# Weight signs carried by a parametric ReLU, and state-times-r matmuls grouped ahead of column-tiled ones

## The chip, the core and the metric

The kernel runs on one core of a Trainium2 chip. The time is device microseconds of that core, from three executions: 1002.29 us median, 1002.23 to 1002.87. One execution, taken by the hardware profiler, gives the trace that this document reads.

## What is computed

A decayed linear attention over 4 x 8 heads of 768 steps and width 48 gives 3072 tokens of 384 features. Two blocks with 2048 hidden features follow, one with a squared ReLU, one with h - tanh(h). The four weight matrices come as float64.

```python
def _attn_ref(r, k, v, w, u):
    for t in range(S):
        cur = np.einsum('bhd,bhe->bhde', u[None] * kt, vt)
        y[:, :, t] = np.einsum('bhd,bhde->bhe', rt, state + cur)
        state = w[None, :, :, None] * state + np.einsum('bhd,bhe->bhde', kt, vt)

def _moe_ref(x, w_in, w_out):
    r = np.maximum(x @ w_in, 0.0)
    return r * r @ w_out

def _moe2_ref(x, w_in, w_out):
    h = x @ w_in
    return (h - np.tanh(h)) @ w_out
```

## The kernel before

The 3072 tokens are six blocks j of 512 tokens: one chunk of 128 time steps, for four batches. A block runs through the attention, then through layer 1. Layer 2 starts when layer 1 is over. A unit of a layer is one slice f of 128 hidden features (16 per block) and one block: `gemm1` (L489, nine matmuls into `h`), an activation (`act1` or `act2`), and `gemm2_1` (L516) or `gemm2_2` (L594). Every fp32 product is a sum of three products of high and low parts, so activations and weights are split in two: `glo` and `xs` are such low parts, made on GpSimd (L507, L549) or VectorE (L583).

**Weights.** The slabs, 32 of them (16 per layer), each hold one f of w_in and w_out as pairs of 32-bit words. `load_w` brings one in (768 KB, buffer `raw`); `conv0` on ScalarE (L84) multiplies the high word, read as float32, by 2^-112, which moves the exponent's offset from float64's to float32's; `conv1` on VectorE puts the words together: L89 shifts the low word, L90 joins the high word shifted left by 3, and L93 adds the sign bit. `conv2` rounds the result on ScalarE (L101) to the high weight part, and GpSimd (L102) subtracts it for the low part; in layer 2 it also asks for the slab five further on. Layer 1's slabs 0 to 2 are converted in the start, slabs 3 to 15 in block 0 (slab f+3 by unit f). Layer 2's slabs 1 to 15 are converted in block 5 of layer 1 (slab f+1 by unit f; slab 0 shortly before). A unit's `gemm1` needs L101 and L102 of its slab.

**Attention.** Blocks 1 to 5 are made while blocks 0 to 4 are in layer 1, in half steps d: half of the heads of one chunk of one batch, eight per block, 40 in all. `att_c(d)` writes the half step's output `y` for two pairs of heads z: L418 multiplies the state `sbd` by r (112 rows by 112 columns of the array), L422 adds the part from within the chunk with two matmuls of 48 columns each, in two places of the array (column tiling). L431 makes the state's addition. Then `att_e(d)` takes `y` out (L448 on ScalarE, L450 on VectorE) and updates the state (L456). GpSimd makes the diagonal of `am` (L320); VectorE fills `am` with L338 or L331.

The order on each engine is written out by hand, in the loop from L762. A unit n first issues `conv2`, then the first half of a unit two or three ahead, then `conv1`, the attention's half step, and the second half of unit n.

```python
        if layer == 1 and j == 0:
            conv1(1, f + 3)
        if att:
            att_c(d)
            att_e(d)
            loads(d)
            pack(d)
        if layer == 1 and j == NB - 1 and 0 < f < NF - 1:
            conv2(2, f - 1)
```

Of the kernel before, what the change touches and what calls it, by code (L numbers as in the profile page):

```python
# [7 lines left out]
F32 = mybir.dt.float32  # L8
# [4 lines left out]
AF = mybir.ActivationFunctionType  # L13
ALU = mybir.AluOpType
# [11 lines left out]
def decay_attention_moe_moe_kernel(  # L26
# [10 lines left out]
    nc = tc.nc  # L37
    NTAU, GP, _, NP, C = rk.shape
# [22 lines left out]
    def bank(i, name):  # L61
        return ps.tile([128, 512], F32, tag=f"bank{i}", name=name)
# [14 lines left out]
    def words(layer, f):  # L77
        raw = raw_t[layer, f]
        return raw[:, :, 0], raw[:, :, 1]

    def conv0(layer, f):
        if f < NF:
            lo, hi = words(layer, f)
            nc.scalar.activation(out=hi.bitcast(F32), in_=hi.bitcast(F32), func=AF.Copy, scale=2.0 ** -112)  # L84

    def conv1(layer, f):
        if f < NF:
            lo, hi = words(layer, f)
            nc.vector.tensor_scalar(out=lo, in0=lo, scalar1=29, scalar2=None, op0=ALU.logical_shift_right)  # L89
            nc.vector.scalar_tensor_tensor(  # L90
                out=lo, in0=hi, scalar=3, in1=lo, op0=ALU.logical_shift_left, op1=ALU.bitwise_or
            )
            nc.vector.scalar_tensor_tensor(  # L93
                out=lo, in0=hi, scalar=0x80000000, in1=lo, op0=ALU.bitwise_and, op1=ALU.bitwise_or
            )

    def conv2(layer, f):
# [20 lines left out]
    sbd = [ac.tile([GP, NP, GP], F32, name=f"sbd{o}") for o in range(TPB)]  # L118
# [10 lines left out]
    rk_t = {}  # L129
# [277 lines left out]
    def att_c(d):  # L407
        i, e = divmod(d, 2)
        j, o = divmod(i, TPB)
        if j not in xt:  # L410
            xt[j] = xp.tile([128, 2, KK, TB], F32R, tag="x", name="xt")
        kn, vn = kv_t[i][:, 0], kv_t[i][:, 1]
        am = am_t.pop(d)
        y = bank(6 if d > 2 * ND and d % 2 else 7, "y")
        yv = y[:, 0:2 * C].rearrange("p (P t) -> p P t", P=2)
        for z in range(2):
            p = 2 * e + z
            nc.tensor.matmul(  # L418
                yv[0:GP, z, :], lhsT=sbd[o][:, p, :], rhs=rk_t[i][:, 0, p, :], start=True, stop=False
            )  # L420
            for a in (1, 0):
                nc.tensor.matmul(  # L422
                    yv[64 * a:64 * a + D, z, :], lhsT=vn[:, 2 * p + a, :], rhs=am[:, 2 * a + z, :],
                    start=False, stop=True,
                )
        pv = y[:, 2 * C:2 * C + 2 * D].rearrange("p (P x) -> p P x", P=2)
        if j != NCH - 1:
            for z in range(2):
                for a in (1, 0):
                    h = 4 * e + 2 * z + a  # L430
                    nc.tensor.matmul(  # L431
                        pv[64 * a:64 * a + D, z, :], lhsT=kn[:, h, :], rhs=vn[:, h, :], start=True, stop=True
                    )
        y_t[d] = (yv, pv)
# [209 lines left out]
    with tc.manual_schedule():  # L644
# [57 lines left out]
        for i in range(TPB):  # L702
# [21 lines left out]
            if i == 0:  # L724
                conv0(1, 0)
                conv1(1, 0)
                conv2(1, 0)
            if i == 1:
                conv0(1, 1)
                att_r(4, G)  # L730
                att_u(5, G)
            if i == 2:
                conv1(1, 1)
            if i == 3:
                conv2(1, 1)
        load_w(1, 3)
        conv0(1, 2)
        rs(4)
        att_d(ND)
# [4 lines left out]
        att_b(ND)  # L744
        att_k(4, G)
        conv1(1, 2)
        att_m(ND)
        load_w(1, 4)
# [13 lines left out]
        for n, (layer, j, f) in enumerate(units):  # L762
# [14 lines left out]
# [5 lines that stand above are left out]
# [108 lines left out]
```

## Time and profile before

| | us |
|---|---|
| median of the runs | 1002.29 |
| profiled execution, own time | 1001.29 |
| its span, first to last instruction | 999.3 |
| PE busy | 943.1 (94%) |
| VectorE (DVE) busy | 777.5 (78%) |
| ScalarE (ACT) busy | 642.6 (64%) |
| GpSimd (POOL) busy | 351.9 (35%) |

Busy time is a mean over stages with different limits. PE is TensorE's matmuls, PEld its weight loads, which lie beside them; matmuls overlap each other in these rows, so their durations add up to more than the time they take. In the chain of waits each matmul counts only with the time that it adds. "issue" is time in which an engine waits for nothing that the profile shows.

### The profile page before, as it was taken

The page shows a single profiled execution, that of the slowest core. Times are in us where ns is not written, and L with a number is a line of the kernel's source. Part 1 is how long each engine was busy: PE and PEld are TensorE (multiplying, and loading weights), DVE is VectorE, ACT ScalarE, POOL GpSimd, SP SyncE. Part 2 cuts the span into 40 slices and gives each one's busy share as a digit, 9 for nine tenths or more (in the row PEclk, how much of TensorE's full clock was granted, in tenths as well). Part 3 has the DMA queues.
Part 4 walks back from the last instruction along what each step waited for, and adds up shares of the span by engine and source line. Part 5 has one row for each costly group of instructions (what it writes and reads, how often), then busy time and mean ns, then how long its engine had stood idle before and what let it go on. Part 6 is the DMA issues. An engine that isn't in the chain of part 4 may idle for free.

```text
span 999.3 us, 14270 instructions
## 1 busy us (share of the span) xinstructions
PE 943.1 (94%) x5036; PEld 788.6 (79%) x5036; DVE 777.5 (78%) x1181; ACT 642.6 (64%) x1157; POOL 351.9 (35%) x267
## 2 busy tenths in 40 slices
PE   6788879999999999999998969999999999999997
PEld 6566657888788888877886758888888898898896
DVE  7999995763674477262189999999999999999996
ACT  3444545554554554544477667888788888888885
POOL 6855665654455455353268911101001001001000
PEclk7999989999999999999999979999999999999999
DMA  8734431211221213110434310010010010100000
GB/s 240 221 126 157 142 110 51 74 56 46 73 88 50 74 51 90 36 47 9 162 128 156 127 53 11 1 53 11 1 53 11 22 33 11 53 11 1 32 1 31
DMA packets 29671, 67.56 MB, mean 68 GB/s; under 512 B 5025, under 2 KB 15137, under 8 KB 29601
## 3 DMA queue, kind: packets, MB, share of 16 engines
q1 hardware_dynamic: 29456, 66.47, 20.9%
q8 instruction: 39, 0.64, 0.3%
q10 hardware_dynamic: 144, 0.20, 0.1%
q14 instruction: 32, 0.25, 0.1%
HBM read 55.25 MB, written 9.44 MB: 65 GB/s over the span
## 4 chain that ended last, share of the span: by engine, by line
PE 68%; DVE 17%; ACT 6%; issue 5%; DMA 2%; POOL 2%; SPq 0%; DVEq 0%; POOLq 0%; ACTq 0%
PE h L489 30%; PE acc L516 16%; PE o L594 15%; DVE raw L90 3%; PE y L422 2%; PE sc L286 2%; PE y L418 2%; DVE raw L89 2%; DVE hy L574 1%; DVE hy L573 1%; DVE hy L572 1%; ACT ghi L582 1%; DVE hy L567 1%; DMA kvt<-in_nat_dram 1%; DVE am L338 1%
## 5 line engine op out<-in xcount | busy, mean ns | idle before, releaser
L489 PE MATMUL h<-xt,w 128*128 128x512 f32 x864 | 217.6, 395 | 6.1 <-ACT w L101 3.1
L489 PE MATMUL h<-xs,w 128*128 128x512 f32 x864 | 215.4, 393 | 0.0
L594 PE MATMUL o<-w,ghi 128*128 128x384 f32 x768 | 198.4, 339 | 7.8 <-ACT x2s L532 4.9
L516 PE MATMUL acc<-ghi,w 128*128 128x512 f32 x576 | 202.5, 406 | 0.0
L489 PEld LDWEIGHTS h<-xt,w 128*128 128x128 f32 x864 | 160.0, 190 | 43.2 <-POOL w L102 5.1
L507 POOL TENSOR_TENSOR glo<-g,ghi 128x512 fp32r<-128x512 f32 x96 | 141.4, 1472 | 146.8 <-ACT ghi L506 110.1
L489 PEld LDWEIGHTS h<-xs,w 128*128 128x128 f32 x864 | 161.2, 188 | 29.5
L594 PEld LDWEIGHTS o<-w,ghi 128*128 128x128 f32 x768 | 141.6, 189 | 18.1 <-ACT x2s L532 5.4
L503 ACT ACTIVATE g<-h 128x512 f32<-128x512 f32 x96 | 57.1, 595 | 152.6 <-PE h L489 151.1
L594 PE MATMUL o<-w,glo 128*128 128x384 f32 x384 | 132.5, 345 | 8.6 <-DVE glo L583 8.3
L516 PEld LDWEIGHTS acc<-ghi,w 128*128 128x128 f32 x576 | 110.8, 192 | 25.8 <-issue 1.3
L549 POOL TENSOR_TENSOR xs<-x2f,xs 128x512 fp32r<-128x512 f32 x18 | 24.1, 1337 | 293.6 <-DVE xs L548 292.4
L516 PE MATMUL acc<-glo,w 128*128 128x512 f32 x288 | 115.0, 399 | 5.3 <-POOL glo L507 5.3
L582 ACT ACTIVATE ghi<-hy 128x512 fp32r<-128x512 f32 x96 | 60.8, 634 | 53.8 <-DVE hy L574 52.7
L102 POOL TENSOR_TENSOR w<-raw,w 128x768 fp32r<-128x768 f32 x32 | 68.0, 2126 | 54.6 <-ACT w L101 54.6
L269 DVE TENSOR_TENSOR fr<-rkt,fr 112x256 fp32r<-112x256 f32 x30 | 39.2, 1305 | 61.7 <-ACT fr L268 60.6
L594 PEld LDWEIGHTS o<-w,glo 128*128 128x128 f32 x384 | 72.5, 189 | 15.5 <-DVE glo L583 13.5
L574 DVE COPY_PREDICATED hy<-mask,th 128x512 f32<-128x512 uint8 x96 | 71.8, 748 | 10.2 <-ACT q L568 0.5
L573 DVE SCALAR_TENSOR_TENSOR hy<-q,hy 128x512 f32<-128x512 f32 x96 | 68.1, 710 | 10.4 <-ACT q L568 0.5
L567 DVE SCALAR_TENSOR_TENSOR hy<-h,y 128x512 f32<-128x512 f32 x96 | 66.3, 690 | 8.6 <-ACT ghi L582 0.5
L320 POOL TENSOR_TENSOR am<-ident,bt 128x512 f32<-128x512 f32 x44 | 50.1, 1139 | 59.6 <-DVE bt L304 56.5
L565 ACT ACTIVATE y<-h 128x512 f32<-128x512 f32 x96 | 56.9, 593 | 21.8 <-PE h L489 21.5
(104 smaller groups left out, 1498.3 us busy)
## 6 DMA issues: line engine op xcount, KB each, us to landing
raw<-in_w_dram SPq DMA_DIRECT2D x32, 768.0 KB, 4.3
rkt<-in_rk_dram SPq DMA_DIRECT2D x23, 448.0 KB, 4.3
kvt<-in_nat_dram SPq DMA_DIRECT2D x23, 384.0 KB, 4.6
x2d<-x2s SPq DMA_DIRECT2D x18, 256.0 KB, 2.3
x2f<-x2d SPq DMA_DIRECT2D x18, 256.0 KB, 2.8
out_dram<-ob SPq DMA_DIRECT2D x24, 192.0 KB, 2.0
rnt<-in_nat_dram SPq DMA_DIRECT2D x23, 192.0 KB, 2.5
xt<-ys SPq DMA_DIRECT2D x120, 16.0 KB, 1.8
```

The lines of the kernel that those rows point to most:

```text
L102: nc.gpsimd.tensor_tensor(d[:, 1], t, d[:, 0].bitcast(F32), op=ALU.subtract)
L320: nc.gpsimd.tensor_tensor(am_t[d].rearrange("p (a z) t -> p a z t", a=2), ident[:, None, None, :].to_broadcast([128, 2, 2, C]), hd.to_broa ...
L489: nc.tensor.matmul(h, lhsT=w_in(layer, f, part, kk), rhs=x[:, xpart, kk, :], start=(n == 0), stop=(n == 3 * KK - 1),)
L503: nc.scalar.activation(out=g, in_=h, func=AF.Relu)
L507: nc.gpsimd.tensor_tensor(lo, g, hi.bitcast(F32), op=ALU.subtract)
L516: nc.tensor.matmul(acc[j][m], lhsT=w_out(1, f, part, m * 128, (m + 1) * 128), rhs=g, start=(f == 0 and n == 0), stop=(f == NF - 1 and n == 2),
L565: nc.scalar.activation(out=y, in_=h, func=AF.Square)
L567: nc.vector.scalar_tensor_tensor(out=hy, in0=h, scalar=PK, in1=y, op0=ALU.mult, op1=ALU.mult)
L573: nc.vector.scalar_tensor_tensor(out=hy, in0=q2, scalar=PD, in1=hy, op0=ALU.add, op1=ALU.mult)
L574: nc.vector.copy_predicated(hy, mask, th)
L582: nc.scalar.activation(out=hi, in_=hy, func=AF.Copy)
L594: nc.tensor.matmul(acc[j][m][:, 0:DM], lhsT=g[:, m * 128:(m + 1) * 128], rhs=w_out(2, f, part, 0, DM), start=(f == 0 and n == 0), stop=(f ...
```

## The change

ScalarE's copy with scale 2^-112 becomes a parametric ReLU with the same scale and a slope of 2^32 for negative numbers. A negative high word so gets 32 added to its exponent, which sets bit 28, and the shift by 3 on VectorE carries bit 28 into the sign's place. L93 is dropped. In `att_c` both L418 matmuls of a half step come first and the four L422 after them; only the first starts the accumulation of its bank.

```diff
     def conv0(layer, f):
-            nc.scalar.activation(out=hi.bitcast(F32), in_=hi.bitcast(F32), func=AF.Copy, scale=2.0 ** -112)
+            nc.scalar.activation(
+                out=hi.bitcast(F32), in_=hi.bitcast(F32), func=AF.Prelu,
+                scale=2.0 ** -112, alpha=2.0 ** 32,
+            )
     def conv1(layer, f):
...
-            nc.vector.scalar_tensor_tensor(
-                out=lo, in0=hi, scalar=0x80000000, in1=lo, op0=ALU.bitwise_and, op1=ALU.bitwise_or
             )
     def att_c(d):
         for z in range(2):
             p = 2 * e + z
             nc.tensor.matmul(
-                yv[0:GP, z, :], lhsT=sbd[o][:, p, :], rhs=rk_t[i][:, 0, p, :], start=True, stop=False
+                yv[0:GP, z, :], lhsT=sbd[o][:, p, :], rhs=rk_t[i][:, 0, p, :], start=(z == 0), stop=False,
+                skip_group_check=True,
             )
+        for z in range(2):
+            p = 2 * e + z
             for a in (1, 0):
                 nc.tensor.matmul(
                     yv[64 * a:64 * a + D, z, :], lhsT=vn[:, 2 * p + a, :], rhs=am[:, 2 * a + z, :],
-                    start=False, stop=True,
+                    start=False, stop=True, skip_group_check=True,
                 )
```

In the changed file L89 and L90 are L92 and L93, and the matmuls of L422, L431, L489, L516 and L594 stand three lines further down. The orders on ScalarE, GpSimd and SyncE are the same before and after, instruction by instruction; ScalarE's has one table load in both, ahead of its first activation (L171).

VectorE before, in block 0: the conversion of a slab, the half step's evacuation behind it, and the next slab.

```order
L250 TENSOR_TENSOR rkt<-rkt,tr 112x256
L89 TENSOR_SCALAR raw<-raw 128x768
L90 SCALAR_TENSOR_TENSOR raw<-raw 128x768
L93 SCALAR_TENSOR_TENSOR raw<-raw 128x768
L450 TENSOR_TENSOR xt<-y,xt 112x2x128
L456 SCALAR_TENSOR_TENSOR sbd_87<-sbd_87,wdec,y 48x48 x4
```

The same place in the change:

```order
L250 TENSOR_TENSOR rkt<-rkt,tr 112x256
L92 TENSOR_SCALAR raw<-raw 128x768
L93 SCALAR_TENSOR_TENSOR raw<-raw 128x768
L453 TENSOR_TENSOR xt<-y,xt 112x2x128
L459 SCALAR_TENSOR_TENSOR sbd_87<-sbd_87,wdec,y 48x48 x4
```

The third operation on `raw` is gone, 32 times; nothing else on VectorE moves.

PE before, one half step between the first half of a unit (`h`) and the second half of another:

```order
L489 MATMUL h<-xt,w_2_556 128x512 x9
L418 MATMUL y<-rkt,sbd_87 112x128
L422 MATMUL y<-am,kvt 48x128 x2
L418 MATMUL y<-rkt,sbd_87 112x128
L422 MATMUL y<-am,kvt 48x128 x2
L431 MATMUL y<-kvt 48x48 x4
```

And in the change:

```order
L492 MATMUL h<-xt,w_2_553 128x512 x9
L418 MATMUL y<-rkt,sbd_87 112x128 x2
L425 MATMUL y<-am,kvt 48x128 x4
L434 MATMUL y<-kvt 48x48 x4
L519 MATMUL acc_610<-ghi,w_1_501 128x512
```

The second L418 now stands ahead of the column-tiled matmuls; the number of matmuls is the same.

## Rows read from the trace of the kernel before

**Rows 1.** Busy time in stretches: length, PE, PEld, DVE, ACT, POOL, clock, DMA, GB/s.
```profile
47.00:150.00 103.00, 85.30 (x465) 61.23 (x461) 95.86 (x134) 48.68 (x78) 61.59 (x40) 0.92 0.41 134
150.00:478.00 328.00, 327.56 (x1862) 265.13 (x1862) 182.07 (x341) 166.02 (x333) 162.26 (x135) 1.00 0.19 57
...
502.70:577.60 74.90, 70.35 (x298) 56.18 (x296) 70.35 (x44) 54.40 (x80) 62.39 (x31) 0.98 0.39 134
577.60:592.00 14.40, 5.19 (x15) 4.53 (x15) 13.61 (x21) 8.84 (x16) 0.00 (x0) 0.65 0.27 91
592.00:990.00 398.00, 392.57 (x1945) 348.36 (x1943) 369.63 (x572) 329.74 (x575) 23.21 (x17) 1.00 0.06 19
```

**Rows 2.** Busy time of L93 alone, in the start and in block 0.
```profile
0.00:47.00 47.00, 3.55 (x3) 0.85 0.82 236
47.00:147.00 100.00, 16.12 (x14) 0.91 0.43 138
```

**Rows 3.** Timeline of VectorE, start and block 0: start, duration, instruction, [idle before, releaser].
```profile
32.95 1.43 DVE L338 COPY_PREDICATED am<-low,sc 128x256 f32<-128x256 uint32 x4 [1.73 <-POOL am L320]
...
66.92 0.96 DVE L93 SCALAR_TENSOR_TENSOR raw<-raw 128x768 uint32<-128x768 uint32 x1
...
79.17 1.91 DVE L93 SCALAR_TENSOR_TENSOR raw<-raw 128x768 uint32<-128x768 uint32 x1
81.00 0.41 DVE L450 TENSOR_TENSOR xt<-y,xt 112x256 fp32r<-112x256 f32 x1
...
84.06 0.78 DVE L338 COPY_PREDICATED am<-low,sc 128x256 f32<-128x256 uint32 x2 [1.24 <-POOL am L320]
```

**Rows 4.** Timeline of GpSimd in block 0, beside the L93 at 79.17.
```profile
78.34 1.93 POOL L507 TENSOR_TENSOR glo<-g,ghi 128x512 fp32r<-128x512 f32 x1
```

**Rows 5.** Timeline of PE in block 0.
```profile
82.37 0.44 PE L418 MATMUL y<-rkt,sbd 112*112 112x128 f32 x2 [3.04 <-DVE sbd L456]
```

**Rows 6.** The chain that ended last, block 1: start, time added, engine, line, count.
```profile
175.88 2.07 PE h L489 x9
...
193.12 2.07 PE h L489 x9
```

**Rows 7.** The same chain, one half step.
```profile
301.79 0.22 PE y L418 x2
302.01 0.36 PE y L422 x4
302.36 0.40 PE y L418 x2
302.76 0.36 PE y L422 x4
...
305.58 0.72 PE sc L286 x6
```

**Rows 8.** Timeline of the weight loads (PEld), the second L418 of a half step.
```profile
171.87 0.27 PEld L418 LDWEIGHTS y<-rkt,sbd 112*112 112x112 f32 x2 [0.18 <-issue]
```

**Rows 9.** Timeline of VectorE in block 5: one slab, and layer 2's first activation.
```profile
547.99 2.21 DVE L89 TENSOR_SCALAR raw<-raw 128x768 uint32<-128x768 uint32 x1
550.30 1.86 DVE L90 SCALAR_TENSOR_TENSOR raw<-raw 128x768 uint32<-128x768 uint32 x1
552.20 2.52 DVE L93 SCALAR_TENSOR_TENSOR raw<-raw 128x768 uint32<-128x768 uint32 x1
...
577.88 0.68 DVE L567 SCALAR_TENSOR_TENSOR hy<-h,y 128x512 f32<-128x512 f32 x1
```

**Rows 10.** Timeline of GpSimd beside that slab.
```profile
547.21 2.57 POOL L102 TENSOR_TENSOR w<-raw,w 128x768 fp32r<-128x768 f32 x1
549.75 1.60 POOL L507 TENSOR_TENSOR glo<-g,ghi 128x512 fp32r<-128x512 f32 x1
551.30 2.58 POOL L102 TENSOR_TENSOR w<-raw,w 128x768 fp32r<-128x768 f32 x1
```

**Rows 11.** Timeline of ScalarE in block 5, a slab that comes late.
```profile
542.85 0.94 ACT L84 ACTIVATE raw<-raw 128x768 f32<-128x768 f32 x1 [4.20 <-DMA raw<-in_w_dram]
```

**Rows 12.** Groups by line, all of the execution: count, busy us, mean ns, idle before.
```profile
L171 ACT ACT_TABLE_LOAD x1 | 1.3, 1283 | 6.9 <-DMA vtab<-in_w_dram 6.9
```

More of the change, by code (lines that the diff above doesn't have):

```diff
@@ L91, in conv1 @@
                 out=lo, in0=hi, scalar=3, in1=lo, op0=ALU.logical_shift_left, op1=ALU.bitwise_or
-            )
-            nc.vector.scalar_tensor_tensor(
-                out=lo, in0=hi, scalar=0x80000000, in1=lo, op0=ALU.bitwise_and, op1=ALU.bitwise_or
             )
```

## The prediction

> **What bounds the kernel now.** I read the busy time by stretches first, since 94% for PE is a mean over stages that end on different things. From 150 to 478 us PE is busy for 327.56 of 328 us [rows 1]: there only less matmul time helps. From 592 to 990 us it is busy for 392.57 of 398 [rows 1], so what comes earlier at 592 comes earlier at the end. In between lie two stretches that PE does not fill: block 0, from 47 to 150 us, with 17.7 us without a matmul, and block 5 with the passage into layer 2, from 502.7 to 592 us, with 4.55 + 9.21 = 13.8 us [rows 1]. In both VectorE is full: 95.86 of 103 us, 70.35 of 74.9, 13.61 of 14.4 [rows 1]. These are the two stretches in which slabs are converted.
>
> Then I read who waits there. In block 0 VectorE's instructions follow each other without a gap but for one of 1.24 us per three units, for GpSimd's `am` [rows 3], and PE waits for VectorE: 3.04 us until L456, which stands behind L89, L90 and L93 in VectorE's order [rows 5]. In block 5 VectorE runs late: layer 2's first activation starts at 577.88 [rows 9], straight behind slab 14's L93.
>
> Then why L93 lasts 0.96 us in one place, 1.91 or 2.52 in another [rows 3, 9]. At 79.17 GpSimd is in L507, which ends at 78.34 + 1.93 = 80.27 [rows 4]; L93 ends 0.81 us after that. In block 5 this holds at every step: L102 ends at 549.78, L89 0.42 us later; L507 ends 1.15 after that, L90 0.81 later, the next L102 1.72 later, L93 0.84 later [rows 9, 10]. The two engines take turns on these instructions: the one that comes second stands until the other's instruction is over. A slab and a unit's L507 so need 0.42 + 0.81 + 0.84 + 1.15 + 1.72 = 4.94 us one behind the other.
>
> **The change, part by part.** The sum is made against the profiled execution's own 1001.29 us (span 999.3), 1.0 us under the median of 1002.29.
>
> *Start.* Two L93 are gone before block 0's first one, which starts just ahead of 47 us: 3.55 - 0.14 = 3.4 us busy [rows 2]. What the first gives falls into a wait, since at 32.95 VectorE has already waited 1.73 us for GpSimd's `am` [rows 3]. The second has no wait behind it: half of the sum, 1.7 us. Bounds 0 and 3.4.
>
> *Block 0.* From there to 146 us 13 more are gone; the last, at 146.74, frees nothing that PE waits for. Their time is 16.12, plus 0.14 of the first that lies before 47 us, less 0.26 of the last: 16.0 us [rows 2]. An instruction starts about 0.08 us before the one ahead of it ends (81.00 against 81.08 [rows 3]), so 16.0 - 13 x 0.08 = 14.9 us of VectorE's order. What is late next? PE's own pace with attention is 193.12 - 175.88 = 17.24 us per three units [rows 6]; VectorE's is now 23.5 (the wait at 84.06 has its like in each such period) and becomes 23.5 - (0.88 + 0.88 + 1.83) = 19.9, still the longer. ScalarE, busy 48.68 of 103 us, and GpSimd, 61.59 [rows 1], have room. So I count all 14.9. Low end: where L93 stood for GpSimd, the next instruction stands instead, and each L93 gives only its own 0.88: 13 x 0.88 = 11.4. High end: the 17.7 us that PE is idle. I take 14.9 because what follows a long L93 is L450 and L456, which read PSUM, and L450 after the long one lasts 0.41 [rows 3]. The Trainium skill (SBUF — State Buffer, "Who interferes with whom") says that VectorE is held by GpSimd only in instructions with two SBUF inputs or in a two-port mode; by it the wait is not passed on to L450, which gives the 14.9, and otherwise 11.4. The turns in block 5 agree with it; no row shows an L450 under a GpSimd instruction.
>
> *Blocks 1 to 4, the matmuls.* In the chain a half step is 0.22 for the first L418 pair of passes, 0.36 for four passes of L422, then 0.40 and 0.36 again [rows 7]. The second L418 is 0.18 dearer than the first, and 0.18 is the time that its weight load stands with nothing shown to wait for [rows 8]: the array has just held column-tiled weights. Grouped, this is paid for nowhere: 0.18 less. A second saving is the other turn: full-width passes with 256 columns add 0.72 / 6 = 0.12 [rows 7], so 128 columns 0.06, four L422 0.24, and the 0.12 left in each 0.36 is the turn to column tiling; one of two goes. Together 0.18 to 0.30 per half step; I take 0.27, nearer the upper end, since both turns are seen in the rows. 32 half steps lie where PE is the bound (blocks 1 to 4; the eight of block 0 are hidden by VectorE): 8.6 us, bounds 5.8 and 9.6.
>
> *Block 5 and the passage.* Before, 14 slabs took turns for 14 x 4.94 = 69.2 of the 74.9 us. After, a slab and an L507 need 4.10, so 57.4 us: 11.8 less, and less than the 70.35 that PE needs [rows 1]. PE becomes the bound again, its 4.55 us of idle time goes, and layer 2's first activation no longer stands behind late slabs but behind its own `h`, so the 9.21 go too, nearly. PE's clock is 0.65 in that last stretch [rows 1]: 5.19 x 0.35 = 1.8 us come back where it is full. So at most 13.8 + 1.8 = 15.6; I take 14. Low end 8: the 9.21, less a part of it that remains. Slab 15 alone, converted in between, gives 0.9 of this.
>
> *ScalarE.* The parametric ReLU does the same 768 elements as the copy. No row shows one; the nearest is L84 itself with 0.94 us [rows 11]. Between nothing and 0.94 more it stays hidden: ScalarE has 74.9 - 54.40 = 20.5 us free for 14 slabs, 1.46 each, in block 5, its tightest place [rows 1]. I count 0.
>
> Sum: 1.7 + 14.9 + 8.6 + 14 = 39.2. 1001.29 - 39.2 = 962.1 for a profiled execution, 1.0 more for a median: **963 us**. All low ends together (0 + 11.4 + 5.8 + 8 = 25.2) give 977, all high ends (3.4 + 17.7 + 9.6 + 15.6 = 46.3) give 956.
>
> **The rivals.**
>
> *The slabs' loads become the bound.* At 542.85 ScalarE stands 4.20 us for a slab that has not landed [rows 11], and everything behind it on ScalarE, the activation of layer 1 included, is late. The load is asked for by the L102 of five slabs before. If the loads stay as late as now, block 5 keeps its 4.55 us and a like delay hits the passage: block 5 gives 5 instead of 14, 972 us. Against it: L102 itself is late now because it takes turns with L93. In block 0 no such wait has a row.
>
> *The second weight load is not hidden.* If the second L418's weights cannot come in while the first L418 runs, the second costs 0.40 as now, and only the turn to column tiling is saved: 0.12 x 32 = 3.8 instead of 8.6, 968 us. The first L418's two passes together add only 0.22, though each loads its weights, and six passes of L286 add 0.72 [rows 7], which speaks against it. The Trainium skill (TensorE: Matmul & The Clock Gate, Part 3, "The mechanism") has loads overlap running matmuls only where the row groups differ; both L418 use the same 112 rows, so that rule gives this rival's 968 us. The rows of L418 and L286 do not bear it out.
>
> *Slower: the parametric ReLU is dear on ScalarE.* Its function could need another table than the copies, squares and tanh around it, and so a load before and one after, 32 times, where now there is one of 1.283 us [rows 12]. The price decides from about 3.5 us per slab: in block 5 ScalarE has 15.95 us free beside PE's 70.35 (1.14 per slab), in block 0, shortened to 88 us, 39.4 (3.0 per slab), and 14 x (3.5 - 1.14) + 13 x (3.5 - 3.0) = 39.5 us eats all the gain. Two loads alone, 2.57 us, add 14 x 1.43 = 20: 983 us, still faster. With as long again for the engine to empty each time, 5.1 us, they add 14 x 3.96 + 13 x 2.1 = 83: 1046 us. Against it: ScalarE's order in the change holds one table load, in the same place. The Trainium skill (ScalarE: Activation LUTs, "What ACT_TABLE_LOAD costs") puts load and drain at 2.66 us; by that two would be 5.3 us per slab and the time about 1051; no run here shows such a drain.
>
> *The half steps in the wrong place.* That the grouping does nothing at all (971.6 us) needs the turns to be unavoidable; the row of 0.18 us speaks against it. I count it to the case of the weight load.
>
> **How the numbers follow.** The forecast, with its own range 956 to 977, has 0.76; the loads 0.11; the weight load 0.07; the dear activation 0.03; 0.03 are left for what no row shows, a third of it slower and a third without effect. The first three all lie within 956 to 977; I widen a little on both sides for the median, to 954 and 978, and leave out well under 2 in 10. A measurement of this kernel can tell about 0.2%, 2 us, from no change. Faster by more than that 0.95, within it 0.01, slower 0.04.
>
> **What would show it.** In the changed profile VectorE's busy time should fall by about 48 us in all, in block 0 each three units should take about 20 us, and PE's idle time between 47 and 135 us should be some 15 us lower. A half step in the chain should read 0.44 for four passes of L418 and about 0.6 for eight of L422; 0.62 for the L418 would be the weight load's case. Layer 1's last block should run without a wait for L507, and layer 2's first L567 should start right behind its `h`. A row for the parametric ReLU over 2 us, or ACT_TABLE_LOAD more than once, would be the slower case; waits of L84 for `raw` of 4 us in block 5, the loads'. The forecast is wrong if VectorE still runs without a gap in block 5, or if PE has new waits in blocks 1 to 4.

## The result and the profile after

| | before | after |
|---|---|---|
| median of the runs, us | 1002.32 | 961.58 (961.38 to 963.43) |
| profiled execution, us | 1001.29 | 961.58 |
| its span, us | 999.3 | 959.6 |
| PE busy, us | 943.1 | 922.6 |
| VectorE busy, us | 777.5 | 742.4 |

The ratio is 0.9597, with a 95% interval of 0.958 to 0.9613. The forecast was 963 us.

First the page of the changed kernel, its busy times and span:

```profile
span 959.6 us, 14238 instructions
...
PE 922.6 (96%) x5036; PEld 784.3 (82%) x5036; DVE 742.4 (77%) x1149; ACT 643.0 (67%) x1157; POOL 346.1 (36%) x267
```

Next, busy time by stretches of the changed kernel, with the columns of [rows 1]. The stretches hold about the same pieces of work as those of [rows 1], at their new times: block 0 with a little of the start ahead of it, blocks 1 to 4, block 5, the passage into layer 2, and layer 2.

```profile
44.60:133.20 88.60, 79.96 (x470) 58.15 (x468) 81.17 (x121) 47.05 (x77) 64.97 (x43) 0.96 0.54 171
133.50:451.00 317.50, 316.88 (x1858) 264.68 (x1860) 190.93 (x340) 165.71 (x331) 160.80 (x134) 1.00 0.19 59
476.00:541.00 65.00, 64.82 (x286) 53.27 (x285) 51.03 (x34) 51.41 (x76) 56.57 (x30) 1.00 0.45 155
541.00:555.00 14.00, 9.64 (x34) 7.89 (x33) 13.24 (x19) 11.48 (x21) 1.87 (x1) 0.76 0.28 94
555.00:953.00 398.00, 391.10 (x1945) 348.58 (x1944) 370.15 (x572) 330.58 (x575) 23.30 (x17) 1.00 0.06 19
```

Block 5 now has 0.18 us without a matmul, where there were 4.55, and VectorE is busy for 51.03 of 65 us there: it is no longer the bound. The passage keeps 14 - 9.64 = 4.4 us of idle PE, where there were 9.2. Block 0 keeps 88.6 - 79.96 = 8.6 where there were 17.7.

Where the time went is read best from the start of the same piece of work in both traces. A unit's second half begins with its first matmul of L516 (now L519), in layer 2 of L594 (now L597):

| start of | before | after | ahead, us |
|---|---|---|---|
| block 0 | 51.50 | 49.13 | 2.37 |
| block 0, last unit | 160.54 | 143.64 | 16.90 |
| block 1 | 166.23 | 149.00 | 17.22 |
| block 5 | 502.69 | 475.97 | 26.72 |
| block 5, last unit | 571.30 | 537.71 | 33.60 |
| layer 2 | 582.59 | 544.81 | 37.78 |
| layer 2, block 1 | 659.46 | 620.61 | 38.84 |
| end of the span | 999.35 | 959.64 | 39.7 |

So 2.4 us came from the start, 14.5 from block 0, 9.8 from block 1 up to block 5, and 13 from there on. The chain that ended last shows what became of a half step in block 1, against [rows 7] (start, time added, engine, line, count):

```profile
168.85 2.07 PE h L492 x9
170.91 0.44 PE y L418 x4
171.35 0.57 PE y L425 x8
171.93 0.18 PE y L434 x8
172.10 2.25 PE acc L519 x9
```

Four passes of L418 add 0.44 us, so the second pair costs as little as the first did, and eight of L425 add 0.57 instead of 0.36 + 0.36. With L434 that is 1.19 us for a half step; before it was 0.22 + 0.36 + 0.40 + 0.36 [rows 7] and 0.18 for L431, 1.52. The last of these in the chain of before:

```profile
303.12 0.18 PE y L431 x8
```

Last, groups by line of the changed kernel (count, busy us, mean ns, idle before):

```profile
L93 DVE SCALAR_TENSOR_TENSOR raw<-raw 128x768 uint32<-128x768 uint32 x32 | 54.3, 1698 | 11.0 <-ACT raw L84 8.5
...
L84 ACT ACTIVATE raw<-raw 128x768 f32<-128x768 f32 x32 | 28.9, 903 | 8.2 <-DMA raw<-in_w_dram 8.2
...
L418 PEld LDWEIGHTS y<-rkt,sbd 112*112 112x112 f32 x160 | 22.5, 177 | 8.3 <-issue 4.5 <-PE h L492 0.6
...
L171 ACT ACT_TABLE_LOAD x1 | 1.3, 1283 | 7.3 <-DMA vtab<-in_w_dram 7.3
```

L84, now the parametric ReLU, takes 0.90 us, and there is still one table load, at the same line [rows 12]. The weight loads of L418 now stand for 4.5 us in all with nothing to wait for, where it was 20.0; [rows 8] showed one such stand of 0.18 us. The group of before:

```profile
L418 PEld LDWEIGHTS y<-rkt,sbd 112*112 112x112 f32 x160 | 25.0, 179 | 23.3 <-issue 20.0
```

### The profile page after: what moved, and what is told of

It reads as the page before. It is cut to its first block, busy times and chain, and to the rows that moved or that the text cites. A ratio compares the mean times of both kernels' runs of the same rounds, so it can differ in the third digit from the quotient of the medians.

```text
span 959.6 us, 14238 instructions
## 1 busy us (share of the span) xinstructions
PE 922.6 (96%) x5036; PEld 784.3 (82%) x5036; DVE 742.4 (77%) x1149; ACT 643.0 (67%) x1157; POOL 346.1 (36%) x267
## 4 chain that ended last, share of the span: by engine, by line
PE 69%; DVE 14%; POOL 5%; issue 5%; ACT 3%; DMA 2%; SPq 0%; DVEq 0%; POOLq 0%; ACTq 0%
PE h L492 31%; PE o L597 17%; PE acc L519 15%; POOL w L102 2%; PE sc L286 2%; PE y L425 2%; DVE hy L575 2%; DVE hy L576 1%; POOL glo L510 1%; PE y L418 1%; DVE raw L93 1%; DVE hy L570 1%; DVE raw L92 1%; DVE hy L577 1%; DMA kvt<-in_nat_dram 1%
## 5 line engine op out<-in xcount | busy, mean ns | idle before, releaser
L597 PE MATMUL o<-w,ghi 128*128 128x384 f32 x768 | 198.1, 339 | 3.7 <-ACT ob L605 2.9
L519 PE MATMUL acc<-ghi,w 128*128 128x512 f32 x576 | 199.2, 400 | 0.0
L510 POOL TENSOR_TENSOR glo<-g,ghi 128x512 fp32r<-128x512 f32 x96 | 135.7, 1414 | 137.7 <-ACT ghi L509 99.8
L597 PEld LDWEIGHTS o<-w,ghi 128*128 128x128 f32 x768 | 141.5, 189 | 14.0 <-ACT ob L605 5.1
L597 PE MATMUL o<-w,glo 128*128 128x384 f32 x384 | 132.1, 344 | 7.6 <-DVE glo L586 7.3
L552 POOL TENSOR_TENSOR xs<-x2f,xs 128x512 fp32r<-128x512 f32 x18 | 25.6, 1420 | 287.7 <-DVE xs L551 287.7
L519 PEld LDWEIGHTS acc<-ghi,w 128*128 128x128 f32 x576 | 109.0, 189 | 24.7 <-ACT g L506 1.1
L519 PE MATMUL acc<-glo,w 128*128 128x512 f32 x288 | 113.5, 394 | 0.8 <-POOL glo L510 0.8
L585 ACT ACTIVATE ghi<-hy 128x512 fp32r<-128x512 f32 x96 | 60.9, 634 | 45.0 <-DVE hy L577 44.1
L597 PEld LDWEIGHTS o<-w,glo 128*128 128x128 f32 x384 | 72.6, 189 | 13.0 <-DVE glo L586 11.1
L577 DVE COPY_PREDICATED hy<-mask,th 128x512 f32<-128x512 uint8 x96 | 75.0, 781 | 9.8
L102 POOL TENSOR_TENSOR w<-raw,w 128x768 fp32r<-128x768 f32 x32 | 67.1, 2098 | 38.6 <-ACT w L101 37.0
L570 DVE SCALAR_TENSOR_TENSOR hy<-h,y 128x512 f32<-128x512 f32 x96 | 66.3, 690 | 10.5 <-ACT th L569 2.0
L576 DVE SCALAR_TENSOR_TENSOR hy<-q,hy 128x512 f32<-128x512 f32 x96 | 66.5, 692 | 10.0
L571 ACT ACTIVATE q<-y,ba 128x512 f32<-128x512 f32 x96 | 69.9, 728 | 0.0
```

The costliest lines, as they stand in the source:

```text
L102: nc.gpsimd.tensor_tensor(d[:, 1], t, d[:, 0].bitcast(F32), op=ALU.subtract)
L510: nc.gpsimd.tensor_tensor(lo, g, hi.bitcast(F32), op=ALU.subtract)
L519: nc.tensor.matmul(acc[j][m], lhsT=w_out(1, f, part, m * 128, (m + 1) * 128), rhs=g, start=(f == 0 and n == 0), stop=(f == NF - 1 and n == 2),
L570: nc.vector.scalar_tensor_tensor(out=hy, in0=h, scalar=PK, in1=y, op0=ALU.mult, op1=ALU.mult)
L571: nc.scalar.activation(out=q1, in_=y, func=AF.Square, bias=p2["ba"], scale=1.0)
L576: nc.vector.scalar_tensor_tensor(out=hy, in0=q2, scalar=PD, in1=hy, op0=ALU.add, op1=ALU.mult)
```

## The experiments

Each row names the ratio to the kernel before on the same chip with its 95% interval. "Ahead" is meant as in the table above, in the profiled execution.

**The two parts apart.** e1 takes the sign alone, from the kernel before:

```diff
-            nc.scalar.activation(out=hi.bitcast(F32), in_=hi.bitcast(F32), func=AF.Copy, scale=2.0 ** -112)
+            nc.scalar.activation(
+                out=hi.bitcast(F32), in_=hi.bitcast(F32), func=AF.Prelu,
+                scale=2.0 ** -112, alpha=2.0 ** 32,
+            )
...
-            nc.vector.scalar_tensor_tensor(
-                out=lo, in0=hi, scalar=0x80000000, in1=lo, op0=ALU.bitwise_and, op1=ALU.bitwise_or
-            )
```

> The sign half of the change alone: the parametric ReLU and two bit operations per slab, the matmuls of a half step in the order of before. Set unit by unit against the kernel before, the changed kernel is 16.9 us ahead when block 0 ends, gains 9.8 us more in blocks 1 to 4, and 13.3 us more from block 5 on (26.7 us ahead before its first stall, 40.0 at the end). Theory (the two halves act in different stretches): this run lacks the 9.8 only, 971.4 us, 971 to 973. Rival (the grouping also helped in block 0, where PE is close behind VectorE): up to 2.5 us more is missing, 973 to 975.

Measured: 969.54 us (969.16 to 972.46), ratio 0.9675 (0.965 to 0.9701), span 967.9. It is ahead by 4.29 at block 0's first unit, by 18.70 at block 1, by 18.67 at block 5 and by 31.4 at the end. So the sign gives nothing at all in blocks 1 to 4, 14.4 in block 0 and 12.7 from block 5 on. That it came out 1.5 us below the lower end of what was expected lies in the start, where it is 1.9 us further ahead than the changed kernel: the executions of the kernels without L93, here and below, are between 2.4 and 5.5 ahead at that unit.

e2 takes the grouping alone:

```diff
-                yv[0:GP, z, :], lhsT=sbd[o][:, p, :], rhs=rk_t[i][:, 0, p, :], start=True, stop=False
+                yv[0:GP, z, :], lhsT=sbd[o][:, p, :], rhs=rk_t[i][:, 0, p, :], start=(z == 0), stop=False,
+                skip_group_check=True,
             )
+        for z in range(2):
+            p = 2 * e + z
```

> The grouping alone: conversion as before, three bit operations. Theory: 32 half steps under a busy PE give 9.8 us, the eight of block 0 nothing, since VectorE is the bound there: 1002.3 - 9.8 = 992.5 us. Rival (VectorE catches up with the gain where the slabs are converted, as it is late in block 5 anyway): part of it is lost again at block 5, 995 to 1002.

Measured: 992.35 us (991.9 to 994.04), ratio 0.9899 (0.988 to 0.9917), span 990.6. It is behind by 0.13 at block 1, ahead by 2.41, 5.24 and 6.70 at blocks 2 to 4, by 8.78 at block 5 and by 8.7 at the end. So block 0 hides the grouping as long as VectorE is the bound there; the 32 half steps after it give 8.9, 0.28 each; and none of it is lost again later. The spans fall by 31.4 (e1) and 8.7 (e2), together 40.1, against 39.7 for the whole change: the parts add up.

**The price of the parametric ReLU.** e3 has the kernel before with the new activation, and keeps the third bit operation, which then ORs a sign that is already there:

```diff
-            nc.scalar.activation(out=hi.bitcast(F32), in_=hi.bitcast(F32), func=AF.Copy, scale=2.0 ** -112)
+            nc.scalar.activation(
+                out=hi.bitcast(F32), in_=hi.bitcast(F32), func=AF.Prelu,
+                scale=2.0 ** -112, alpha=2.0 ** 32,
+            )
```

> The parametric ReLU takes the copy's place, but the third bit operation stays, which then sets a sign that is set already; matmuls as before. It prices the ScalarE side by itself. Theory (same price as the copy): 1002.3 us, L84 at about 0.91 us, one table load. Rival (a dearer activation, hidden in the changed kernel behind shorter VectorE work): over 1004 us, or a longer L84.

Measured: 1003.16 us, ratio 0.9996 (0.9985 to 1.0008). Its L84 takes the same mean as before, and it has one table load. The dear activation falls.

**What the third operation costs: work or a turn.** e4 adds to the changed kernel a third bit operation on 16 of the 768 columns, a 48th of what L93 did before:

```diff
+            nc.vector.scalar_tensor_tensor(
+                out=lo[:, 0:16], in0=hi[:, 0:16], scalar=0x80000000, in1=lo[:, 0:16],
+                op0=ALU.bitwise_and, op1=ALU.bitwise_or
+            )
```

> The changed kernel with a third bit operation again, but on 16 of the 768 columns: its own work is nearly nothing, its turn against GpSimd is back. Theory (the two engines take turns, a whole instruction at a time): where GpSimd is busy it lasts as long as GpSimd's instruction still runs, 1 us and more in the long places of block 0 and at most slabs of block 5, and about 0.1 us elsewhere; the time is 966 to 973 us. Rival (they share the way to SBUF by the amount moved): 0.1 us everywhere, 961.6 + 3 = at most 965 us.

Measured: 969.28 us (968.23 to 970.3), ratio 0.9665 (0.9646 to 0.9685), 7.7 us above the changed kernel, or 6.8 by the two ratios. In this kernel the new operation is L96, and the old L507 is L514. Its group:

```profile
L96 DVE SCALAR_TENSOR_TENSOR raw<-raw 128x16 uint32<-128x16 uint32 x32 | 24.7, 773 | 1.1
```

Two of them in block 0, in VectorE's timeline (start, duration, instruction), and GpSimd beside them:

```profile
70.63 0.18 DVE L96 SCALAR_TENSOR_TENSOR raw<-raw 128x16 uint32<-128x16 uint32 x1
...
72.05 2.47 DVE L93 SCALAR_TENSOR_TENSOR raw<-raw 128x768 uint32<-128x768 uint32 x1
74.55 1.13 DVE L96 SCALAR_TENSOR_TENSOR raw<-raw 128x16 uint32<-128x16 uint32 x1
75.60 0.41 DVE L457 TENSOR_TENSOR xt<-y,xt 112x256 fp32r<-112x256 f32 x1
```

```profile
71.82 1.88 POOL L106 TENSOR_TENSOR w<-raw,w 128x768 fp32r<-128x768 f32 x1 [2.04 <-ACT w L105]
73.70 1.95 POOL L514 TENSOR_TENSOR glo<-g,ghi 128x512 fp32r<-128x512 f32 x1
```

With GpSimd idle, at 70.63, sixteen columns take 0.18 us. At 74.55 they take 1.13 and end at 75.68, just after GpSimd's L514 ends at 73.70 + 1.95 = 75.65. L93 ahead of them ends at 74.52, 0.82 us after GpSimd's L106. All 32 follow this: 13 start while GpSimd runs nothing and take 0.18 us, and the other 19 take 0.85 to 1.75 us and end 0.03 or 0.04 us after an instruction of GpSimd. So what the removed operation cost was in part the wait for a turn, and that wait does not shrink with its size. From block 0's first unit to block 1's this kernel gains 8.75 us, the changed kernel 17.22 - 2.37 = 14.85.

The Trainium skill (SBUF — State Buffer, "Who interferes with whom") says that a VectorE instruction with two SBUF inputs contends with a GpSimd instruction that reads SBUF. These rows agree: L96 and L93 have two. L457 behind them has one input in PSUM and takes 0.41 us, but GpSimd's instruction ends 0.05 us after it starts, so it tests nothing here; the changed kernel's L453 does (below, at block 0).

**The array's turns.** In e5 the state's addition (the four matmuls of the old L431, column-tiled too) goes ahead of the two L418, so that a half step needs a turn to column tiling and back twice again, while the two L418 still stand together:

```diff
+        pv = y[:, 2 * C:2 * C + 2 * D].rearrange("p (P x) -> p P x", P=2)
+        if j != NCH - 1:
+            for z in range(2):
...
         for z in range(2):
...
-        pv = y[:, 2 * C:2 * C + 2 * D].rearrange("p (P x) -> p P x", P=2)
-        if j != NCH - 1:
-            for z in range(2):
```

> The changed kernel with the state's addition (the column-tiled 48-wide matmuls) ahead of the two L418 and not behind the L422. The two L418 still stand together, but the array turns to column tiling and back twice per half step, as before the change. 24 of the half steps under a busy PE have this addition. Theory (a turn there and back costs the 0.31 us): 961.6 + 24 x 0.31 = 969 us. Rival (the gain comes from the two L418 standing together, whose second weights load behind the first's run): 961.6 us, unchanged within 1 us.

Measured: 968.42 us (966.4 to 969.0), ratio 0.9654 (0.9632 to 0.9677). Blocks 1 to 3 now gain 0.16, 0.16 and -0.18 us on the kernel before; block 4, whose half steps make no state addition, gains 2.08. Its chain in block 1, where L421 is the state's addition, L426 the product with the state and L433 the part within the chunk:

```profile
184.67 2.07 PE h L492 x9
186.74 0.32 PE y L421 x8
187.06 0.62 PE y L426 x4
187.68 0.57 PE y L433 x8
188.25 2.26 PE acc L519 x9
```

The same eight passes of the state's addition add 0.32 us behind a full-width matmul and 0.18 behind a column-tiled one; the four passes of the state product add 0.62 behind a column-tiled matmul and 0.44 behind a full-width one. A turn to column tiling so costs 0.14, a turn back 0.18, 0.32 together. That it pays to have the two L418 side by side as such falls. The Trainium skill (TensorEngine Tiling (Array Packing), "Key Properties") says that a change of the tiling mode drains TensorE; the chain agrees that a change costs time, 0.14 and 0.18 us.

**What holds the passage into layer 2.** The changed kernel still loses 4.4 us there. VectorE's timeline of the changed kernel, from the last slab of layer 1's time on:

```profile
533.92 2.46 DVE L93 SCALAR_TENSOR_TENSOR raw<-raw 128x768 uint32<-128x768 uint32 x1
538.34 0.69 DVE L570 SCALAR_TENSOR_TENSOR hy<-h,y 128x512 f32<-128x512 f32 x1 [1.96 <-ACT th L569]
...
541.13 2.37 DVE L577 COPY_PREDICATED hy<-mask,th 128x512 f32<-128x512 uint8 x1
543.39 0.54 DVE L92 TENSOR_SCALAR raw<-raw 128x768 uint32<-128x768 uint32 x1
543.97 0.96 DVE L93 SCALAR_TENSOR_TENSOR raw<-raw 128x768 uint32<-128x768 uint32 x1
544.84 0.68 DVE L570 SCALAR_TENSOR_TENSOR hy<-h,y 128x512 f32<-128x512 f32 x1
```

And PE's timeline at the same place, the first matmuls of L597:

```profile
531.59 2.20 PE L492 MATMUL h<-xs,w 128*128 128x512 f32 x9
...
544.81 0.62 PE L597 MATMUL o<-w,ghi 128*128 128x384 f32 x2 [0.82 <-ACT x2s L535]
548.97 0.69 PE L597 MATMUL o<-w,glo 128*128 128x384 f32 x1 [3.54 <-DVE glo L586]
```

Layer 2's first `h` is there at 533.8, but its first activation starts on VectorE at 538.34, after 1.96 us of waiting for ScalarE. ScalarE had stood for loads of layer 2's slabs, as the waits from 500 to 562 us show (us in all, times, longest):

```profile
ACT raw L84 <- DMA raw<-in_w_dram: 7.3, 6, 2.5
...
PE o L597 <- DVE glo L586: 3.5, 1, 3.5
```

So the loads were the first suspect. e6 gives them a sixth buffer and asks for each a unit earlier:

```diff
-        pool, n = (cv, 3) if layer == 1 or f % 5 < 3 else (p2["pool"], 2)
+        pool, n = (cv, 3) if layer == 1 or f % 6 < 3 else (p2["pool"], 3)
...
-            if layer == 2 and f + 5 < NF:
-                load_w(2, f + 5)
+            if layer == 2 and f + 6 < NF:
+                load_w(2, f + 6)
...
-                    for q in range(5):
+                    for q in range(6):
                         load_w(2, q)
```

> The changed kernel with six buffers instead of five for layer 2's slabs, each load asked for one unit earlier. In the changed kernel's block 5 ScalarE still stands 7.3 us for slabs that have not landed, and layer 2's first activation is late by about 4 us behind that. Theory (the loads are what is left of the stall): these waits go and the time falls by 2 to 4 us, 957.5 to 959.5. Rival (the passage is bound by VectorE's own order, the first low part standing behind the second unit's activation): the waits go, the time stays at 961.6 within 1 us.

Measured: 961.15 us (960.21 to 962.22), ratio 0.9589 (0.9571 to 0.9607): the changed kernel's time within what can be told. ScalarE's waits for loads at L84 fall from 8.2 to 1.8 us in all, and the first activation of layer 2 starts 4 us earlier, in VectorE's timeline of e6:

```profile
534.17 0.69 DVE L570 SCALAR_TENSOR_TENSOR hy<-h,y 128x512 f32<-128x512 f32 x1 [0.40 <-ACT th L569]
```

But the wait of PE stands as it was, in PE's timeline of e6:

```profile
547.29 0.69 PE L597 MATMUL o<-w,glo 128*128 128x384 f32 x1 [3.47 <-DVE glo L586]
```

Of the 1.7 us that the second unit of layer 2 is earlier than in the changed kernel, 0.8 were there when block 5 began, and all of it is gone again by the end. Where the 4 us of the first activation go, VectorE's next rows in e6 show, and GpSimd beside them:

```profile
536.18 1.60 DVE L576 SCALAR_TENSOR_TENSOR hy<-q,hy 128x512 f32<-128x512 f32 x1
...
540.02 2.23 DVE L92 TENSOR_SCALAR raw<-raw 128x768 uint32<-128x768 uint32 x1
...
543.16 0.68 DVE L570 SCALAR_TENSOR_TENSOR hy<-h,y 128x512 f32<-128x512 f32 x1
```

```profile
537.20 4.63 POOL L102 TENSOR_TENSOR w<-raw,w 128x768 fp32r<-128x768 f32 x2
```

From its first L570 to its second VectorE takes 8.99 us here and 6.50 in the changed kernel: L576 and L92, which took 0.69 and 0.54 us there, now come second in a turn with GpSimd. So VectorE's second L570 starts at 543.16, 1.7 us ahead of the 544.84 of the changed kernel and no longer 4. Late loads were real and did not set the time.

e8 then issues the first unit's low part ahead of the second unit's activation:

```diff
         gemm1(layer, j, f)
+        if n == NB * NF + 1:
+            act2_late()
         (act1 if layer == 1 else act2)(j, f)
```

> The changed kernel with one thing moved: the first high and low part of layer 2's activation (L585 on ScalarE, L586 on VectorE) are made ahead of the second unit's activation and not behind it. In the changed kernel PE stands 3.5 us for that low part after its first two matmuls of L597. Theory (this wait is what is left of the passage): it goes and the end comes 2 to 3.5 us earlier, 958 to 959.5. Rival (VectorE has no gap from there on, so its order, the same work in another sequence, sets the end): the wait goes, the time stays at 961 within 1 us.

Measured: 962.3 us (961.03 to 964.0), ratio 0.9601 (0.9586 to 0.9615). PE's wait for L586 is gone, and another of its size stands at L597's first matmul, in PE's timeline of e8:

```profile
546.12 1.01 PE L597 MATMUL o<-w,ghi 128*128 128x384 f32 x2 [3.97 <-ACT x2s L535]
```

The first unit's high part (L585) now stands in ScalarE's order ahead of the second unit's activation, and waits there for VectorE, in ScalarE's timeline of e8; L535, which empties the last accumulators, comes behind both:

```profile
542.15 0.63 ACT L585 ACTIVATE ghi<-hy 128x512 fp32r<-128x512 f32 x1 [2.58 <-DVE hy L577]
...
545.48 1.57 ACT L535 ACTIVATE x2s<-acc 128x512 f32<-128x512 f32 x3
```

So the low part comes earlier and the emptied accumulators come later: L535 started at 544.14 in the changed kernel. e9 has both edits, and c1 is the changed kernel once more, with no edit, on the same chip:

> Both at once: six buffers for layer 2's slabs, which took ScalarE's waits for them but only 0.8 us of the time, and the first low part early. If each alone is covered by the other, both together give more than the sum: theory, 957 to 958.5 us. Rival (VectorE's order sets the end): what the sixth buffer alone gave, 960.5 to 961.5.

> The changed kernel itself once more, on the same chip as the two above, so that differences of 1 us can be read: 961.6 us.

Measured: e9 960.32 us (959.12 to 963.46), ratio 0.9582 (0.9564 to 0.9599); c1 961.12 us (959.9 to 963.28), ratio 0.9587 (0.9571 to 0.9603). The two can't be told apart. In e9 layer 2's second unit starts 44.99 us ahead, in c1 40.84; then PE waits 2.27 us for that unit's low part, and at layer 2's second block both are 40.62 ahead. From layer 2's first activation on VectorE has no wait over 0.5 us in e6, e8, e9 and c1. That fits the rival of e6, e8 and e9, VectorE's order as what sets the end; no run shortened that order itself. No version here beats the changed kernel by more than a measurement can tell.

**Layer 2's own bound.** VectorE is busy for 370.15 of 398 us in layer 2. In e7 ScalarE takes five sixths of one of its operations, the cast L551:

```diff
-        nc.vector.tensor_copy(xs[j][:, 0, m, :], t)
+        (nc.scalar.activation(out=xs[j][:, 0, m, :], in_=t, func=AF.Copy) if j else nc.vector.tensor_copy(xs[j][:, 0, m, :], t))
```

> The changed kernel with layer 2's input rounding (L551, 0.34 us of VectorE's order, 15 times) on ScalarE for blocks 1 to 5. It asks what paces layer 2. Theory (VectorE does: its six instructions take 4.19 us per unit against PE's 4.18, and the roundings come on top): 961.6 - 15 x 0.34 = 956.5 us. Rival (PE paces it and VectorE is only as late as it may be, or ScalarE's order is delayed by the 0.5 us each): 961 us or more.

Measured: 965.63 us (965.38 to 966.8), ratio 0.9636 (0.9618 to 0.9653), 4 us slower than the changed kernel. It enters layer 2 well (41.50 ahead at the second unit) and then loses about 1 us per block: 39.78 at block 2's first unit, 38.68 at block 4's, 36.83 at the last unit; the changed kernel loses nothing there. The reason stands in VectorE's rows. GpSimd's L552, the subtraction that follows each cast, now follows ScalarE's cast, and starts 0.6 us before an L575, which has two SBUF inputs. VectorE's timeline of e7, and GpSimd's:

```profile
645.33 1.28 DVE L575 SCALAR_TENSOR_TENSOR hy<-q,hy 128x512 f32<-128x512 f32 x1
```

```profile
644.77 1.30 POOL L552 TENSOR_TENSOR xs<-x2f,xs 128x512 fp32r<-128x512 f32 x1 [49.83 <-PE h L492]
```

All 15 of the L575 beside an L552 last 1.23 to 1.28 us in e7 and 0.80 to 0.96 in the changed kernel, where one without GpSimd lasts 0.68. So VectorE lost 15 casts and got 15 longer waits for a turn. From its ninth to its fifteenth L570 of a block it now takes 26.9 us where it took 26.1; over five blocks that is the 4 us. PE's waits for VectorE's low parts follow, from 560 to 950 us, in e7 and then in the changed kernel (us in all, times, longest):

```profile
PE o L597 <- DVE glo L586: 4.2, 12, 1.2
```

```profile
PE o L597 <- DVE glo L586: 2.0, 2, 1.6
```

So e7 did not shorten VectorE's order, as it was meant to, but lengthened it, and the time rose with it. That speaks for VectorE as layer 2's pace rather than against it; no run gave VectorE less to do in layer 2.

## Why the prediction was right

The sum was 39.2 us for a profiled execution; 39.7 came off. That the two are so close is in part luck: the terms are off by about +0.7, -0.4, +0.9 and -1 us and cancel, and c1, the same kernel, ends 41.4 us ahead. By its terms:

**Start, 1.7 counted, 2.4 measured.** The bounds were 0 and 3.4. This term is the least certain one: the same kernel was 5.4 us ahead at that unit in its second execution (c1). In the profiled execution of the changed kernel GpSimd waits 9.3 us for `rnt` to land, in c1 5.8, before 5.5; so when the first inputs land is part of it.

**Block 0, 14.9 counted, 14.5 measured** (14.4 in e1). The period of three units was forecast as 19.9; units 6 to 9 take 108.53 - 88.93 = 19.6. In the executions of e1, e5 to e9 and c1 the way from block 0's first unit to block 1's gives 14.1 to 16.2 us, and start and block 0 together 17.2 to 19.7; so the two terms are told apart to some 2 us only. The choice between 14.9 and 11.4 went the right way. VectorE's timeline in the changed kernel, then GpSimd's:

```profile
72.10 2.46 DVE L93 SCALAR_TENSOR_TENSOR raw<-raw 128x768 uint32<-128x768 uint32 x1
74.48 0.41 DVE L453 TENSOR_TENSOR xt<-y,xt 112x256 fp32r<-112x256 f32 x1
74.82 0.89 DVE L459 SCALAR_TENSOR_TENSOR sbd<-sbd,wdec,y 48x48 f32<-48x48 f32 x4
...
77.54 0.79 DVE L338 COPY_PREDICATED am<-low,sc 128x256 f32<-128x256 uint32 x2 [1.24 <-POOL am L320]
```

```profile
73.75 1.96 POOL L510 TENSOR_TENSOR glo<-g,ghi 128x512 fp32r<-128x512 f32 x1
```

L453 behind the long L93 is as short as L450 was [rows 3], and it runs wholly beside a GpSimd instruction, as it does again at 94.08 and 113.69; so the wait is not handed on to it. The trace of before had such a case too, which the prediction did not use: an L450 at 463.09 takes 0.29 us beside an L507 that runs from 462.80 to 464.09. VectorE's only waits in block 0 are four of the known 1.24 for `am`.

**Blocks 1 to 4, 8.6 counted, 9.5 to 9.8 measured** (8.9 in e2), between the bounds 5.8 and 9.6, or just above. PE has one wait there, of 0.5 us. The mechanism held, and the value was mis-sized: I took 0.27 per half step, measured are 0.28 (e2) to 0.30. The step that was short is the turn to column tiling. I estimated it at 0.12 from full-width passes that are twice as wide; e5 shows 0.14 for it. With the 0.18 of the turn back, which I had read rightly, that is 0.32.

**The weight load's rival fell.** Four passes of L418 add 0.44, not 0.62. The Trainium skill's rule (TensorE: Matmul & The Clock Gate, Part 3, "The mechanism"), by which loads overlap running matmuls only where row groups differ, is not borne out by this row: all four use the same 112 rows, and a load of 0.18 us (L418's group above) is longer than the 0.11 that a pass adds, so it lies beside the passes.

**Block 5 and the passage, 14 counted, 13 measured.** Block 5 itself did as forecast: VectorE is no longer full, and PE stands for 0.18 us. The step that was too large is "the 9.21 go too, nearly": 4.4 us of them stay. I wrote that layer 2's first activation would stand behind its own `h` only; it starts 4.5 us after it, behind a slab's L93 until 536.38 and then behind ScalarE. So the rival of the late loads was there as a wait (six waits of L84, the longest 2.5 us and not 4), but e6 shows that it is not what the 4.4 us hang on. They hang on the order of ScalarE and VectorE up to the first low part and the emptied accumulators: with the loads early (e6) VectorE loses in turns what it had gained, and with the low part early (e8) the emptied accumulators come late instead.

Up to layer 2's second block, 38.84 - 26.72 = 12.1 us were gained. PE's idle time accounts for 13.8 - 0.2 - 4.4 = 9.2 of it. Some 1 us is clock: granted 0.98 of 70.35 and 0.65 of 5.19 us before, 1.00 of 64.82 and 0.76 of 9.64 after, which is 3.2 against 2.3 us short of full speed. The remaining 2 us were not split further.

**Two forecasts for the profile were wrong.** VectorE's busy time should have fallen by 48 us and fell by 35. The 48.3 us of L93 are gone, but other instructions now come second in a turn: 32 of the 44 L250 last over 1 us, where it was 20, and each of these ends 0.28 or 0.29 us (0.55 in three) after a GpSimd instruction. L250 takes 51.3 us where it took 39.3, L249 34.5 for 28.5, and the cast 12.6 for 7.6; L275 fell from 43.7 to 37.1. One is in the rows above: the L577 at 541.13 lasts 2.37 us, beside a GpSimd L102, where its like lasts 0.78 on average. So busy time falls by less than the work removed, while the time fell by what the path said.

And PE's idle time in block 0 should have fallen by 15 us and fell by 17.7 - 8.6 = 9.1. The other part of the gain is busy time: 85.30 us became 79.96, 5.3 less. PE is idle for 10% of the stretch instead of 17%, and the granted clock rose from 0.92 to 0.96, a mean between the two levels of 1.2 and 2.4 GHz. An estimate from these rows puts the clock at 0.08 x 85.3 - 0.04 x 80.0 = 3.6 us and the grouping at 8 x 0.3 = 2.4. I counted the gain along VectorE's order, which was right, and looked for it in one row of PE, which shows only a part.

**ScalarE, nothing counted, nothing measured:** L84 takes 0.90 us, one table load, and e3 is 0.9996 of the kernel before.

## What to carry to other kernels

Price an instruction on an engine that takes turns with another by the path it stands on and by the turn it may wait for, not by its size: sixteen columns of 768 cost some 7 us here, where the whole operation cost 992.35 - 961.58 = 30.8. Taking work off such an engine can make it slower where that shifts the other engine's turn, as in e7. Where matmuls of one half step use the array in two ways, put those of one way together and count the turns; here each cost 0.14 or 0.18 us beside matmuls that add 0.02 to 0.11. A wait that disappears (the loads in e6, the low part in e8) is no gain until the next one behind it has been looked at.

## What was not expected of the hardware

- One VectorE operation of 16 columns takes 0.18 us with GpSimd idle and 1.13 us beside a GpSimd instruction; 32 of them take 24.7 us.
- The turn to column tiling (0.14 us) and the turn back (0.18 us) are two separate prices, and both show in one chain (e5).
- With the casts of five blocks moved from VectorE to ScalarE, the kernel became slower by 4 us (e7): 15 other VectorE instructions now stand for GpSimd and last 1.23 to 1.28 us instead of 0.80 to 0.96.
- Executions of kernels with the same start differ there by up to 3 us (block 0's first unit at 46.1 to 49.1 us in two executions of the changed kernel), so one profiled execution can't settle a term of 1 or 2 us that lies in the start.
